# Six denser rows of quarter-array products per chunk, and V loaded behind the score blocks

## The chip, the cores and the metric

The kernel runs on one core of a Trainium2 chip. The metric is device microseconds of one execution; lower is better. Times below are medians of repeated runs, and one execution was also recorded by the hardware profiler.

## The reference

The program is a delta-rule attention block (4 batches, 8 heads, 768 tokens, head dimension 48) whose output feeds a feed-forward layer with SiLU (384 to 2048 to 384):

```python
for t in range(S):
    kt, vt, bt = (k_n[:, :, t], v[:, :, t], beta[:, :, t, None])
    y[:, :, t] = np.einsum('bhd,bhde->bhe', q[:, :, t], state)
    v_old = np.einsum('bhde,bhd->bhe', state, kt)
    state = state + bt[:, :, :, None] * np.einsum('bhd,bhe->bhde', kt, vt - v_old)
...
h = x @ w_in
g = h * (1.0 / (1.0 + np.exp(-h)))
return (g @ w_out).astype(np.float32)
```

Here `k_n` is k over its norm, and x is y with the heads side by side: 3072 tokens by 384.

## The kernel before, in words

The 768 tokens are cut into 6 chunks of 128, and each chunk into two halves of 64. All 32 heads of a chunk are worked together, in two groups g of two batches. Matrices of 64 x 64 sit in the four quarters of TensorE's array, so four small products run side by side; a product of float32 is two passes, and each pass is a weight load and a matmul, four instructions in all.

For chunk c the work is in three parts.

- `prepare(c)`, `block_steps`, `invert(c)`: `turn_blocks` (VectorE) brings k and q into transposed form, `score` (L516, with `mask`) makes the score matrices, `block_out` and `block_in` carry 32 x 32 diagonal blocks through memory into g, and `invert` inverts them on VectorE in 31 steps (L614, L619, L622). The result goes through memory again into xe and xi (`read_up`).
- `solve(c)`: `merge` (L769, 32 x 32 products) builds the rest of the inverse; per half, `keys` (L815) takes the state's prediction off V (tile vf), `inner` (L827) multiplies by the inverse into z, `old` (L893) starts the output from the state, `update` (L847) moves the state on and `new` (L906) finishes the output from z. ScalarE copies z out of the accumulators; `copy_out` and `move` bring the output into xT, the input of the feed-forward layer, partly by DMA.
- `feed_forward(c, hf)`: `hidden` (L1028) and `combine` (L1135), full-array products in half-steps of 3 or 4 matmuls. There are 60 half-steps a chunk.

[...] The last loop of the kernel alternates the parts. `go(solving)` emits the next piece of `solve`, up to its next `yield`, and `run(n)` emits n half-steps of feed-forward work of the chunk before. What stands between two `run`s is called a row here. `together` interleaves the products of its arguments one by one. All DMAs of SyncE's queue keep the order in which they are emitted (`in_line`).

The rows of `solve(c)` were: merge; keys; merge; inner and old of both groups; update and new of both groups; an empty one (copies only); keys; inner and old; update and new. `follow(c)` issues the loads of q for the next chunk, and `load_v` those of V: 8 DMAs of 96 KB. `size(c, g)` (L454) scales V on GpSimd. `lengths(c)` makes the norms of k, by squares on GpSimd and sums on VectorE.

The functions that the diff touches, and what calls them:

## Time and profile before

| what | us |
|---|---|
| median of 3 runs | 653.4 |
| their range | 652.0 to 657.42 |
| span of the profiled execution | 653.9 |
| TensorE products busy | 631.9 |
| TensorE weight loads busy | 552.0 |
| VectorE busy | 398.4 |
| ScalarE busy | 214.0 |
| GpSimd busy | 91.0 |

The span runs from the first to the last instruction of the one profiled execution. A time of its own, measured without the profiler, is not to be had, so the span is set beside the median. Chunk 0 and 1 and the weights' preparation take the first 180 us, chunks 2 to 5 the next 400, and the feed-forward layer of the last chunk the rest. Between the first merges of chunks 3, 4 and 5 pass 98.2 and 97.8 us.

### The profile page before, as it was taken

How to read it: one execution, taken by the hardware profiler on the slowest of the kernel's cores; microseconds unless marked ns; L12 is line 12 of the kernel's file. 1: busy time of each engine (PE TensorE's matmuls, PEld its weight loads, DVE VectorE, ACT ScalarE, POOL GpSimd, SP SyncE). 2: the span in 40 equal slices, each digit the busy share in tenths (PEclk: the TensorE clock that was granted, in tenths of full speed). 3: DMA queues.
4: the chain of work that ended last, by engine and by line, in shares of the span. 5: the costliest groups of instructions: out<-in, count | busy, mean ns of one | idle time of the engine just before them, and what ended most of it. 6: DMA issues, size and time to landing. Idle time of an engine off the chain costs nothing.

```text
span 653.9 us, 21366 instructions
## 1 busy us (share of the span) xinstructions
PE 631.9 (97%) x9416; PEld 552.0 (84%) x9416; DVE 398.4 (61%) x911; ACT 214.0 (33%) x497; POOL 91.0 (14%) x92
## 2 busy tenths in 40 slices
PE   7888999999999999999999999999999999999997
PEld 5576778756789988989989989989989989889997
DVE  5874689997774986443987444986444974103112
ACT  2454664332352122451122452122451122441111
POOL 5023631235101020010020010020002000000000
PEclk9968999999999998999999999999999999999999
DMA  9966634350267324167424168424073024100101
GB/s 135 211 154 191 211 72 106 97 96 3 59 146 143 62 73 60 36 142 130 79 73 59 35 146 141 63 73 60 22 148 81 2 72 60 41 13 1 25 0 25
DMA packets 145676, 54.70 MB, mean 84 GB/s; under 512 B 117152, under 2 KB 138912, under 8 KB 145584
## 3 DMA queue, kind: packets, MB, share of 16 engines
q1 hardware_dynamic: 143136, 52.93, 39.4%
q8 instruction: 74, 1.21, 0.8%
q10 hardware_dynamic: 2448, 0.41, 0.4%
q14 instruction: 18, 0.15, 0.1%
HBM read 40.14 MB, written 11.01 MB: 78 GB/s over the span
## 4 chain that ended last, share of the span: by engine, by line
PE 86%; DVE 6%; DMA 3%; issue 2%; ACT 2%; SPq 1%; POOL 0%; DVEq 0%; POOLq 0%
PE phid L1028 34%; PE px L1135 15%; PE py L1135 11%; PE po L1063 7%; PE pa L516 3%; PE pz L827 3%; DVE rank L614 2%; PE pu L847 2%; PE pyc L906 2%; PE ph L815 2%; DVE x L619 2%; PE pt L487 1%; PE pw L335 1%; PE pyc L893 1%; DMA kb<-in_k_dram 1%
## 5 line engine op out<-in xcount | busy, mean ns | idle before, releaser
L1028 PE MATMUL phid<-xT,w_in 128*128 128x256 f32 x1152 | 259.9, 383 | 1.3 <-DMA xT<-part 1.3
L1028 PEld LDWEIGHTS phid<-xT,w_in 128*128 128x128 f32 x1152 | 216.7, 191 | 33.2 <-issue 2.7
L1038 ACT ACTIVATE gT<-phid 128x512 f32<-128x512 f32 x88 | 52.6, 597 | 149.5 <-PE phid L1028 142.7
L614 DVE SCALAR_TENSOR_TENSOR rank<-g,step,x 128x31 f32<-128x31 f32 (+15 forms) x124 | 49.7, 401 | 38.0 <-DMA g<-blocks 34.6
L1117 DVE TENSOR_TENSOR sums_of_g<-gT 128x384 f32<-128x384 f32 (+1 forms) x60 | 31.7, 548 | 56.7 <-ACT gT L1038 46.1
L1135 PE MATMUL px<-sums_of_w,sums_of_g 128*128 128x192 f32 x320 | 56.8, 329 | 0.0
L1135 PE MATMUL py<-w_out,sums_of_g 128*128 128x192 f32 x320 | 56.8, 329 | 0.0
L1135 PEld LDWEIGHTS px<-sums_of_w,sums_of_g 128*128 128x128 f32 x320 | 52.2, 190 | 0.5
L1135 PEld LDWEIGHTS py<-w_out,sums_of_g 128*128 128x128 f32 x320 | 52.2, 190 | 0.4
L619 DVE TENSOR_TENSOR x<-x,rank 128x31 f32<-128x31 f32 (+15 forms) x124 | 42.5, 342 | 4.3
L454 POOL TENSOR_TENSOR vf<-vf,n_slot 128x768 f32<-128x768 f32 x10 | 15.0, 1516 | 172.6 <-DMA vf<-in_v_dram 126.9
L475 DVE STREAM_TRANSPOSE kq<-stage 128x512 f32<-128x512 f32 x28 | 28.5, 1116 | 11.1 <-DMA stage<-in_q_dram 11.1
L531 ACT COPY xT<-pyc 48x128 f32<-48x128 f32 (+2 forms) x126 | 32.7, 260 | 1.6
L1135 PE MATMUL px<-w_out,gT 128*128 128x192 f32 x160 | 29.7, 341 | 0.0
L1135 PEld LDWEIGHTS px<-w_out,gT 128*128 128x128 f32 x160 | 28.1, 200 | 0.5
L1135 PE MATMUL px<-sums_of_w,gT 128*128 128x192 f32 x160 | 28.4, 329 | 0.0
L1135 PE MATMUL py<-w_out,gT 128*128 128x192 f32 x160 | 28.4, 329 | 0.0
L827 PEld LDWEIGHTS pz<-vf,xi 64*64 64x64 f32 x768 | 25.4, 141 | 3.2 <-issue 2.9
L827 PE MATMUL pz<-vf,xi 64*64 64x48 f32 x768 | 27.0, 226 | 0.0
L1135 PEld LDWEIGHTS py<-w_out,gT 128*128 128x128 f32 x160 | 26.1, 190 | 0.3
L537 POOL COPY g<-x 64x256 f32<-64x256 f32 x4 | 5.0, 1247 | 153.3 <-DVE x L622 153.3
L1135 PEld LDWEIGHTS px<-sums_of_w,gT 128*128 128x128 f32 x160 | 26.1, 190 | 0.2
(195 smaller groups left out, 829.5 us busy)
## 6 DMA issues: line engine op xcount, KB each, us to landing
vf<-in_v_dram SPq DMA_DIRECT2D x48, 96.0 KB, 2.9
out_dram<-o SPq DMA_DIRECT2D x42, 96.0 KB, 2.2
w_out<-in_moe_w_in_dram SPq DMA_DIRECT2D x4, 768.0 KB, 4.6
sums_of_w<-in_moe_w_out_dram SPq DMA_DIRECT2D x4, 768.0 KB, 5.9
blocks<-ap SPq DMA_DIRECT2D x44, 64.0 KB, 1.9
g<-blocks SPq DMA_DIRECT2D x5, 512.0 KB, 4.1
kb<-in_k_dram SPq DMA_DIRECT2D x12, 192.0 KB, 4.8
kb<-in_k_dram SPq DMA_DIRECT2D x24, 96.0 KB, 4.3
```

The costliest lines, as they stand in the source:

```text
L454: pin(nc.gpsimd.tensor_tensor(out=vf, in0=vf, in1=of, op=ALU.mult))
L475: pin(nc.vector.transpose(out=kqs[c, b][:, :, j, :].rearrange("p a (i m) -> p a m i", i=T), in_=src.rearrange("p a (m d) -> p a m d", d=D) ...
L516: pin(nc.tensor.matmul(pa[e][half, p * n * W : (p + 1) * n * W], lhsT=kq[rows, p, 0, half], rhs=kq[rows, p, js[0] : js[-1] + 1, half], sta ...
L531: return pin(nc.scalar.copy(to, of))
L614: pin(nc.vector.scalar_tensor_tensor(out=tv, in0=g[:, 0:m, m : m + 1].to_broadcast([P, m, n]), scalar=step[:, m : m + 1], in1=x[:, m : m + ...
L619: yield pin(nc.vector.tensor_tensor(out=x[:, 0:m, m:T], in0=x[:, 0:m, m:T], in1=tv, op=ALU.add))
L827: yield pin(nc.tensor.matmul(pz[rows, n * D : (n + 1) * D], lhsT=xis[g][rows, u * H + 2 * p + e, :], rhs=vfs[c][rows, hf, g * HB + u, p, : ...
L1028: pin(nc.tensor.matmul(ph[:, j * GT : (j + 1) * GT], lhsT=w_in[:, a, (2 * f + j) * P : (2 * f + j + 1) * P], rhs=xTs[c, hf][:, a, :], star ...
L1038: pin(nc.scalar.activation(out=hidden_of(c, hf, f), in_=ph[:], func=ACTF.Silu, scale=-0.5 if in_blocks(c) else 0.5))
L1063: pin(nc.tensor.matmul(pos[i][:, 0:DM], lhsT=hidden_of(0, hf, f // 2)[:, at : at + C], rhs=w_outs[f // HFF][:, f % HFF, :], start=(f == 0) ...
L1117: pin(nc.vector.tensor_tensor(out=sums_of_g[:, k, fs], in0=of[0], in1=of[1], op=op))
L1135: pin(nc.tensor.matmul(to, lhsT=at, rhs=quarter(f, *b) if isinstance(b, tuple) else sums_of_w[b][:, f], start=start and f == 0, stop=f == ...
```

## The change

For chunks 2 to 5 `solve` makes fewer and longer rows. keys of the first half and the first merge form one row; a new function `half_chunk` puts inner and old of both groups and update and new of both groups into one row, with update and new of one group side by side in place of the same kind of both groups. The scores of all four batches are one row in place of two. The last half of chunk 5, which has no update, makes new of both groups together.

The V of the next chunk was loaded in the middle of `solve`; it is now loaded in `prepare`, behind `block_in`. `size` moves from the start of `prepare` to after the inversion. The numbers of half-steps between rows are set anew: 10 in place of 16 in `solve`, 5 in place of 4 between `solve` and the end of the scores, 12 or 14 in place of 8 or 10 behind the inversion.

```diff
+    def half_chunk(c, hf):
+
+        for g in range(2):
+            together(inner(c, g, hf), old(c, g, hf))
+        if c == NCH - 1 and hf == 1:
+            together(new(c, 0, hf), new(c, 1, hf))
+        else:
+            for g in range(2):
+                together(update(c, g, hf), new(c, g, hf))
+        copy_out()
...
+        if c > 1:
+            together(keys(c, 0, 0), keys(c, 1, 0))
+            together(merge(c, 0, False), merge(c, 1, False))
+            yield
+            together(merge(c, 0, True), merge(c, 1, True))
+            yield
+            half_chunk(c, 0)
+            yield
+            copy_out()
+            move()
+            yield
+            together(keys(c, 0, 1), keys(c, 1, 1))
+            follow(c)
+            yield
+            half_chunk(c, 1)
+            yield
+            copy_out()
+            move()
             return
...
             if hf == 1:
                 together(keys(c, 0, 1), keys(c, 1, 1))
-                if c > 1:
-                    follow(c)
                 yield
             for g in range(2):
                 together(inner(c, g, hf), old(c, g, hf))
             if hf == 1:
-                if c == 1:
-                    follow(c)
-                load_v(c + 1)
+                follow(c)
...
         if in_blocks(c):
-            for g in range(2):
-                size(c, g)
...
                     turn_blocks(c, b, 1)
-                if g == 1:
-                    for b in range(HB):
-                        scored(b)
                 yield
-            for b in range(HB, B):
+            for b in range(B):
                 scored(b)
             block_in(c)
+            load_v(c)
             yield
             return
...
-            for n in range(9):
+            for n in range(6):
                 go(solving)
-                run((2, 2, 2, 2, 1, 1, 2, 2, 2)[n])
-                if n == 5:
+                run((2, 2, 1, 1, 2, 2)[n])
+                if n == 2:
                     pieces = chained(pieces, feed_forward(c, 0), feed_forward(c, 1))
...
-            for _ in ready:
-                run(2)
-            run(6)
+            go(ready)
+            run(3)
+            go(ready)
+            run(8)
...
+            for g in range(2):
+                size(c + 1, g)
             after = lengths(c + 2) if c + 2 < NCH else iter(())
-            for _ in range(8 if c == 1 else 10):
+            for _ in range(12 if c == 1 else 14):
                 run()
-                go(after, 4)
+                go(after, 3)
```

More of the change, by code (lines that the diff above doesn't have):

```diff
@@ L984, in solve @@
             return
+        if c > 1:
[16 more added lines that the diff above has]
+            move()
+            return
         together(merge(c, 0, False), merge(c, 1, False))
```

## The prediction

> **What bounds the kernel now.** First the page: the busy shares, and the queue that carries instructions.

> ```profile
> PE 631.9 (97%) x9416; PEld 552.0 (84%) x9416; DVE 398.4 (61%) x911; ACT 214.0 (33%) x497; POOL 91.0 (14%) x92
> ...
> q8 instruction: 74, 1.21, 0.8%
> ```

> TensorE is busy 97% of the span, so only its own stream and its few waits can move the time. It runs 9416 products and 9416 weight loads, 18,832 instructions, and q8 brought them in 74 packets: 16 KB and some 256 instructions each. I come back to that.

> Second, the chain that ended last, in order of time, cut to 240 to 320 us and 343 to 400 us.

> ```profile
> 247.60 1.25 PE py L769 x80
> 248.85 4.48 PE px L1135 x16
> 254.41 2.80 PE px L1135 x16
> ...
> 312.06 2.60 PE py L1135 x16
> ...
> 363.80 1.08 PE pu L847 x64
> 364.88 0.89 PE pyc L906 x57
> 365.77 0.21 issue
> 365.98 0.34 PE pyc L906 x7
> ...
> 378.89 0.95 PE pyc L906 x64
> ```

> Sixteen full-array records of L1135 take 2.60 us among their like (312.06) and 2.80 between two rows of quarter products (254.41): a return to the full array costs 0.20. A row of 64 quarter records alone takes 1.08 (pu), a second one right behind the first 0.95 (378.89): 14.7 ns a record and 0.14 for the way in. One row more or less between full-array work is therefore 0.34 us. The merge row at 247.60 began late, and the first full-array group behind it takes 4.48 in place of 2.80. At 365.77 it waits 0.21 us for nothing but "issue".

> Third, the waits of TensorE's products in the window 195 to 580 us, chunks 2 to 5:

> ```profile
> PE py L769 <- DMA xe<-low: 1.5, 2, 0.8
> PE phid L1028 <- DMA xT<-part: 1.3, 2, 0.8
> PE pyc L906 <- issue: 0.2, 1, 0.2
> ```

> That is all there is to gain from waits: xe in chunk 2, xT in chunk 5, one "issue".

> **What the change saves.** (1) Rows. In the order of the built program a chunk had 8 rows of small products in solve and 2 of scores; it has 5 and 1. Sixteen rows less (4 x 4; chunk 5 loses 3 in solve and chunk 2 to 5 one each of scores) by 0.34 is 5.4 us. The products are the same, and kinds that follow each other cost nothing extra: pyc starts 1.08 after pu, which is the row's own length. Bound: 0 to 0.14 for keys beside merge, at most 0.6 in all; I take 0.

> (2) The xe wait of chunk 2: the merge row takes 2.11 against 1.22 in the other chunks, 0.9; another 0.9 lies before it (the full-array work there takes 51.67 for 39 half-steps of 1.30); the slow group behind it has 4.48 less 2.80, 1.7: 3.5. The half-steps of feed-forward work between scores and merge rise from 8+23+8 to 8+23+12 at c = 1, by 4 x 1.30 = 5.2 us; in the later chunks from 41 to 45. Behind xe stands the scores' way through memory, which SyncE's queue sets:

> ```profile
> 283.56 6.17 SPq L188 DMA_DIRECT2D vf<-in_v_dram  x8
> ...
> 292.43 4.11 SPq L886 DMA_DIRECT2D xT<-part  x5
> 296.64 4.28 SPq L101 DMA_DIRECT2D blocks<-ap  x8
> ```

> SyncE issues back to back from 270.98 to 300.92, so the 8 V issues (6.17 us) hold up 4 stores, 5 xT copies and 8 block writes. Behind block_in they precede only the k loads, which are wanted a chunk later. V itself is then wanted by size(), 30 us on. size() moves on GpSimd behind x L622: 2 x 1.46 us, and the four squares behind it make VectorE's sums of squares wait some 3 us; next late are sums_of_g, which feed products 6 half-steps (7.8 us) later. So it costs 0; without that cover it would be 3 a chunk.

> (3) The xT wait of chunk 5: 4.71 us for a group that is 2.80 elsewhere, 1.9. Before, the backlog shrinks by one half-step a chunk (61 run, 60 made) until chunk 5's first hidden product meets its own copies; after, it is 60 and 60 and a half chunk lies between. Gone: 1.9. (4) The issue wait at 365.77 and the row's other delay, 0.5, belong to that old order: gone.

> Saved: 5.4 + 3.5 + 1.9 + 0.5 = 11.3 us.

> **What it costs: the z copies.** inner, old, update and new now follow without feed-forward work between. ScalarE copies z for g = 0 at 360.11 for 0.48, with the row begun at 358.91; ready at 1.68, wanted when old of g = 1 ends, at 1.88. z for g = 1 ends at 2.62 and is wanted at 1.88 + 0.94 = 2.82. Both fit, by 0.2. Only in the last half, where new runs for both g at once, it is wanted at 1.88: a wait of 0.8. If ScalarE were 0.5 later (one activation in its way), each of 8 halves would lose 0.3.

> **What it costs: instructions.** These are stretches of the opening, by busy time:

> ```profile
> 37.90:40.25 2.35, 2.35 (x127) 2.25 (x128) 1.81 (x3) 1.45 (x4) 0.00 (x0) 0.50 0.74 275
> 40.25:41.73 1.48, 0.00 (x0) 0.00 (x0) 1.20 (x3) 0.36 (x1) 1.34 (x1) 0.50 0.08 18
> 52.05:55.60 3.55, 3.54 (x126) 2.79 (x127) 1.21 (x3) 1.04 (x2) 0.00 (x0) 1.00 0.65 213
> 55.60:57.19 1.59, 0.00 (x1) 0.00 (x0) 1.15 (x3) 0.42 (x1) 1.01 (x1) 1.00 0.54 98
> ```

> From the end of one "issue" wait TensorE runs 255 or 253 instructions (first two brackets: products and weight loads) and waits again, 1.48 and 1.59 us, with nothing on either of its rows. Counted in the built program, with a constant offset of 62, the three later waits (151.06, 181.54, 365.98) fall exactly on 20, 26 and 46 times 256. So TensorE holds the block it runs and one more; a dense row eats a block faster than the next arrives. From one block's first instruction to the next one's, where it waited, passed 3.83 (37.90 to 41.73), 5.14 (52.05 to 57.19), and 3.56 at the made row (362.42 to 365.98).

> A made row had 256 instructions and 32 slow ones on either side. A half_chunk has 512 in a row: 256 x 7.33 ns = 1.88 us a block. By my count the first block boundary falls 77, 138, 248, 54, 164, 225 and 79 instructions into the seven full halves, so the second always falls inside too. Its wait is the pace less 1.88. In slow stretches q8's packets start when, by my count, 46 instructions of the old block are left, 0.34 us in a dense row; so I take a pace of 3.4, just below the nearest row (3.56): 1.5 each, 10.5 in all. Bounds: 0.9 (3.56 less that lead twice, 2.9, and a tenth off) and 2.2 (the mean of 3.56 and 5.14, less the lead). Two more places: the keys-and-merge row of chunk 4 has a whole block in it (1.2 us at merge speed, 4.2 ns an instruction): 2.2; and in chunk 3 three boundaries fall from the second merge to the end of the half, 10.2 us of pace on 7.7 of work, 1.0 beyond the 1.5. Sum 13.7, bounds 8 and 20.

> [...]

> **What it costs: the clock.** Windows around three waits:

> ```profile
> 245.50:248.90 3.40, 1.89 (x131) 1.40 (x130) 2.96 (x15) 0.60 (x1) 0.00 (x0) 1.00 1.24 173
> 248.90:252.30 3.40, 3.40 (x11) 3.40 (x12) 3.22 (x10) 1.16 (x2) 0.00 (x0) 0.50 0.90 100
> 566.30:569.70 3.40, 2.14 (x10) 1.21 (x8) 1.11 (x4) 0.61 (x3) 0.00 (x0) 1.00 0.28 69
> 569.70:573.20 3.50, 3.45 (x134) 3.01 (x135) 0.00 (x0) 1.03 (x3) 0.00 (x0) 1.00 0.44 105
> ```

> With 1.51 us idle in 3.40 the granted clock (third from the end) is 0.50 in the next stretch; with 1.26 idle it stays 1.00. A wait of 1.5 is at that edge, and may be split between two stretches. Of the nine waits I let three cost it, at the 1.68 of the row at 248.85: 5.0. Bounds: 0, and seven times 1.68, 11.8. [...]

> **Sum.** -11.3 + 0.8 + 13.7 + 5.0 = +8.2. The span is 653.9; the median of the runs 653.4, so I count 0.5 off: 653.9 + 8.2 - 0.5 = 661.6, told as 661.5.

> **Rivals.** (a) The blocks arrive in time, the other side: one mechanism, instruction supply in the halves, decides at a pace of 1.9 us a block. Then -11.3 + 0.8: 643. For it: from 256 to 290 us seven boundaries pass without a wait. Against: they lie 4.6 us apart there, and the stretches from 37.90 on show what happens when they are nearer. Chance 0.12. (b) The waits come but stay near 1 us and the clock holds: -11.3 + 0.8 + 8 to 12.5: 651 to 655. For it: the opening's pace was taken beside 200 GB/s of other traffic, the halves run beside less. Against: 3.56 at 4 GB/s. Chance 0.23. (c) Nearly every wait costs clock, or loads of q beside the second halves slow the blocks: 20 + 8: 668 to 672. Chance 0.12. (d) The stream is less dense than its order says because z comes late: up to 8 x 0.3 = 2.4 on (a), 645; it would hide in the waits otherwise. Chance 0.03. The forecast, 656 to 667, keeps 0.50.

> **Numbers.** A measurement of this kernel can tell about 1% (646.9 and 659.9) from no change. Faster: (a) and (d) almost whole, 0.13. Slower: (c) and three quarters of the forecast, 0.50. Same: the rest, 0.37. The range 649 to 671 leaves out (a), (d) and some of (c); the forecast's own is 656 to 667.

> **What would show it.** Right: "issue" waits of 1 to 2 us in pu or pyc, once in each of seven halves, 333 instructions or so after its start, and one in the merge of chunk 4; no xe and no xT wait; clock of 0.50 in a few stretches; chunk period (merge to merge) near 99 us against 97.7. Each row's group of 16 still 2.80. Wrong: halves that last 3.9 us would make the instruction term 0 and the period 95.1 (97.7 less 1.3 for the half-step and 1.36 for four rows); waits on ScalarE's z in pu would mean my margin of 0.2 was none; a wait on xe would mean the block chain did not get shorter.

## The result, and the profile after

The changed kernel takes 663.31 us (median of 6 runs, 661.14 to 669.99), the kernel before in the same comparison 657.25 (652.0 to 658.92). The ratio is 1.0136, with a 95% interval of 1.0091 to 1.018: slower. The profiled execution of the changed kernel has a span of 662.1 us, 8.2 above the 653.9 of before; the two medians differ by 6.1.

The busy times and the chain's shares of the profile page, after:

```profile
PE 631.2 (95%) x9416; PEld 555.6 (84%) x9416; DVE 400.4 (60%) x911; ACT 214.3 (32%) x497; POOL 91.3 (14%) x92
...
PE 92%; issue 3%; DMA 2%; DVE 1%; ACT 1%; SPq 0%; DVEq 0%
```

TensorE is busy as long as before (631.2 against 631.9); the 8.2 us are time in which it does nothing. The waits of its products in 185 to 590 us say where (total, times, longest):

```profile
PE pu L847 <- issue: 5.4, 4, 2.0
PE pyc L906 <- issue: 3.5, 3, 1.5
PE py L769 <- issue: 2.2, 2, 1.6
PE pyc L893 <- issue: 1.1, 1, 1.1
PE pyc L906 <- ACT z L531: 0.5, 1, 0.5
```

The waits for xe and xT that led this list before are gone. Ten waits that end with nothing but "issue" stand in their place, 12.2 us in all, eight inside the halves and two in rows of keys and merge. One such wait in the chain, in the second half of chunk 2, whose row began at 272.62:

```profile
275.68 0.07 PE pu L847 x2
275.75 2.00 issue
277.75 0.20 PE pu L847
```

Products of the same row run up to it and behind it. And the clock, in windows around that wait and around the one of 1.63 us in chunk 4's row of keys and merge (the granted clock is third from the end):

```profile
275.66:279.07 3.41, 1.41 (x65) 1.25 (x60) 0.76 (x2) 2.14 (x7) 0.00 (x0) 1.00 0.73 153
279.07:282.48 3.41, 3.41 (x11) 3.23 (x11) 0.87 (x3) 0.86 (x3) 0.00 (x0) 0.50 0.78 147
...
453.15:456.56 3.41, 1.78 (x145) 1.57 (x137) 1.10 (x3) 0.00 (x0) 0.00 (x0) 1.00 0.02 5
456.56:459.97 3.41, 3.41 (x12) 3.41 (x12) 2.75 (x5) 1.49 (x3) 0.00 (x0) 0.50 0.03 7
```

Each wait is followed by 3.41 us at half clock. Between 180 and 660 us these are the only two such stretches.

### The profile page after: what moved, and what is told of

It reads as the page before. It is cut to its first block, busy times and chain, and to the rows that moved or that the text cites. A ratio compares the mean times of both kernels' runs of the same rounds, so it can differ in the third digit from the quotient of the medians.

```text
span 662.1 us, 21399 instructions
## 1 busy us (share of the span) xinstructions
PE 631.2 (95%) x9416; PEld 555.6 (84%) x9416; DVE 400.4 (60%) x911; ACT 214.3 (32%) x497; POOL 91.3 (14%) x92
## 3 DMA queue, kind: packets, MB, share of 16 engines
q8 instruction: 74, 1.21, 0.8%
## 4 chain that ended last, share of the span: by engine, by line
PE 92%; issue 3%; DMA 2%; DVE 1%; ACT 1%; SPq 0%; DVEq 0%
PE phid L1054 38%; PE px L1161 16%; PE py L1161 12%; PE po L1089 6%; PE pa L516 3%; PE pz L827 3%; PE pu L847 2%; PE ph L815 2%; PE pyc L906 1%; PE pt L487 1%; PE pw L335 1%; PE pyc L893 1%; DMA kb<-in_k_dram 1%; PE py L769 1%; PE px L769 1%
## 5 line engine op out<-in xcount | busy, mean ns | idle before, releaser
L1143 DVE TENSOR_TENSOR sums_of_g<-gT 128x384 f32<-128x384 f32 (+1 forms) x60 | 30.0, 521 | 62.2 <-ACT gT L1064 51.5
L1161 PE MATMUL py<-w_out,sums_of_g 128*128 128x192 f32 x320 | 59.8, 338 | 0.0
L1161 PEld LDWEIGHTS py<-w_out,sums_of_g 128*128 128x128 f32 x320 | 54.3, 195 | 0.4
L852 DVE TENSOR_TENSOR state<-state,pu 128x384 f32<-128x384 f32 x22 | 11.8, 552 | 32.2 <-PE pu L847 17.6
L1161 PE MATMUL px<-w_out,gT 128*128 128x192 f32 x160 | 27.6, 326 | 0.0
L526 DVE TENSOR_TENSOR ap<-pa,above 128x256 f32<-128x256 f32 x44 | 16.4, 418 | 17.6 <-ACT ap L531 13.8
L551 POOL MEMSET x<- 128x1024 f32 x4 | 3.8, 952 | 168.3 <-DMA xT<-part 75.4
L1161 PEld LDWEIGHTS px<-w_out,gT 128*128 128x128 f32 x160 | 26.6, 190 | 0.5
```

The costliest lines, as they stand in the source:

```text
L526: pin(nc.vector.tensor_tensor(out=to, in0=of, in1=above[:].unsqueeze(1).to_broadcast([P, NP, W]), op=ALU.mult))
L1143: pin(nc.vector.tensor_tensor(out=sums_of_g[:, k, fs], in0=of[0], in1=of[1], op=op))
L1161: pin(nc.tensor.matmul(to, lhsT=at, rhs=quarter(f, *b) if isinstance(b, tuple) else sums_of_w[b][:, f], start=start and f == 0, stop=f == ...
```

## The experiments

**Same rows, other block boundaries.** The edit, in the opening:

```diff
     busy(3)
+    pd = bank(CC, "pw")
+    for _ in range(48):
+        pin(nc.tensor.matmul(pd[0:T, 0:T], lhsT=ident[0:T, 0:T], rhs=ident[0:T, 0:T], start=True, stop=True))
     for b in range(B):
         square(0, b)
```

> The changed kernel with 48 products of 32x32 in the opening, whose results nobody reads: 192 TensorE instructions more ahead of everything, and nothing else. Theory 1, blocks of 256 instructions: the total of the issue waits in chunks 2 to 5 stays near 13 us, but every one moves by 192 instructions. With 3.65 us from one block to the next the row of keys and merge should wait some 2.1 us in chunk 2 (0.59 in the changed kernel) and 2.1 in chunk 5 (none there), and not in chunk 4 (1.63 there); the halves wait once each, 192 instructions earlier or 64 later in their order. Theory 2, z or any other data or position in the row: the same places and sizes as in the changed kernel, because nothing but the count ahead of them has changed. The time is within 4 us of the changed kernel's.

Measured: 667.2 us (one run), span 665.4. Of the waits of its products in 185 to 590 us:

```profile
...
PE py L769 <- issue: 3.3, 2, 1.9
PE px L769 <- issue: 1.6, 1, 1.6
...
PE pyc L906 <- ACT z L531: 0.5, 1, 0.5
```

The two waits of py are now in chunk 2 (1.4 us, expected 2.1) and chunk 5 (1.9, expected 2.1), and chunk 4, which had 1.63, has none. Nothing but the count of instructions ahead of the row has changed, so the place of these waits follows that count. The halves say it to the instruction. This is the number of product records that ran in a row before its wait:

| row (first and second: the halves) | changed kernel | shifted |
|---|---|---|
| chunk 2, keys and merge | 136 | 168 |
| chunk 2, first | 165 | 197 |
| chunk 2, second | 197 | 229 |
| chunk 3, first | 123 and 251 | 155 |
| chunk 3, second | 155 | 187 |
| chunk 4, first | 209 | 241 |
| chunk 4, second | 241 | 145 |
| chunk 5, first | 167 | 199 |
| chunk 5, last (waits for z) | 130 | 130 |

A record of a product has a weight load beside it (9416 of each), so 32 records later are 64 instructions, and 96 earlier are 192: the shift, modulo 256. The only wait on data, z in the last half, stays where it was, at 0.5. So neither z nor a fixed place in the row makes the others. From the start of the second half of chunk 4 to its wait, changed and then shifted (products alone; each count has one record of the full-array work before):

```profile
476.64:480.41 3.77, 3.77 (x242) 1.00 0.74 163
...
477.53:479.80 2.27, 2.27 (x146) 1.00 0.39 95
```

Not as foreseen: this half waits only 0.12 us in the shifted run, where I expected a wait in each of the seven, and 1.6 us are lost in the second merge of chunk 5, right behind the other. With pu (4.5), pyc (4.0) and a full-array product behind a row (0.9) the total is 14.3, not 13.

**The suspected cost by itself.** The kernel before, with a probe row in the four inversions:

```diff
+                if n == 12:
+                    pds = [bank(A, "pw"), bank(CC, "pw")]
+                    for i in range(128):
+                        i1, i2 = i % 2, i // 2 % 2
+                        i3 = slice(W * (i // 4 % 8), W * (i // 4 % 8) + W)
+                        i4 = HALVES[i1]
+                        pin(nc.tensor.matmul(
+                            pds[i2][HALVES[i1 ^ i2], i3], lhsT=ident[i4, i4], rhs=ident[i4, i4],
+                            start=True, stop=True, skip_group_check=True,
+                        ))
+                    run()
...
-            for _ in range(8 if c == 1 else 10):
+            for _ in range(7 if c == 1 else 9):
```

In the second version `if i == 64: run()` stands in the loop in place of the `run()` behind it.

> The kernel before with a probe: once in each of the four inversions, between two half-steps, 128 products of 64x64 on the identity into two banks, in one row: 512 TensorE instructions that wait for no data and that nobody reads. Theory 1, blocks: each of the four rows takes 128 x 14.7 ns = 1.9 us x 2 = 3.8 us plus one wait for nothing but issue of 1.2 to 1.8 us in it. Theory 2, the waits of the halves came from z or from copies: no wait in any probe row, 3.8 us each.

> The same probe, cut into two rows of 64 products (256 instructions) with one half-step of full-array work between. Theory 1: no issue wait over 0.4 us in any of the eight rows; each takes 1.9 to 2.0 us with its way in. The time is under that of the probe in one row by some 4 x (1.5 + 0.3) less 4 x 0.34, 6 us, and by up to 1.7 more for each stretch of half clock that the waits bring. Theory 2: no difference but the four rows more, 1.4 us slower.

Measured: 683.37 us in one row (span 681.4), 673.52 in two (span 671.6), one run each. The chain through the first probe, in one row:

```profile
225.61 2.94 PE pw L1524 x186
228.55 1.37 issue
229.91 1.27 PE pw L1524 x67
```

and cut in two:

```profile
220.43 2.02 PE pw L1526 x128
222.46 1.50 PE py L1135 x8
223.96 2.02 PE pw L1526 x128
```

The four long rows wait 1.37, 1.31, 0.90 and 1.13 us and last 5.1 to 5.6; of the eight short ones seven last 2.02 or 2.03 and one 2.19, with no wait. Nothing here waits for data. One half-step of 1.50 us between them was enough. Two of the four waits lie in the 1.2 to 1.8 expected, two below it. The difference of the times, 9.9 us, holds waits in the opening too (5.6 against 1.5 us in pl L733), which fell otherwise in these two executions and which I do not explain.

The traces hold two more signs of the same cause. In the eleven profiles (both kernels and all experiments) TensorE's products wait 120 times, behind 30 us and for over 0.15 us, for nothing but issue. Counted in the trace (products, weight loads and the sequencer's records of TensorE, and the same 63 added in every run), the instruction behind each of these 120 waits has a number that is a multiple of 256; not one of the 74 waits for another engine or a DMA stands at such a place. And each of the 120 ends 1.19 to 1.81 us after a packet of 16 KB on the instruction queue q8 had ended, while the waits on data end 1.2 to 25 us after one.

**The halves cut in two.**

```diff
-            half_chunk(c, 0)
+            half_inner(c, 0)
+            yield
+            half_outer(c, 0)
...
-                run((2, 2, 1, 1, 2, 2)[n])
-                if n == 2:
+                run((2, 2, 1, 1, 1, 2, 1, 1)[n])
+                if n == 3:
...
-            for _ in range(12 if c == 1 else 14):
+            for _ in range(11 if c == 1 else 13):
```

The same cut is made in the second half; `half_inner` and `half_outer` are the two parts of `half_chunk`.

> The changed kernel, but each half of chunks 2 to 5 is cut into two rows again: inner with old (256 instructions), one half-step of feed-forward work, then update with new (256). 60 half-steps a chunk as in the changed kernel, 11 of them in solve. Theory 1, instruction blocks: no stretch of a half is longer than a block any more, so the eight waits for nothing but issue inside the halves (10.0 us in the profile of the changed kernel) go or stay under 0.4 us each, with the 0.3 us by which each stretched its row besides and one of the two stretches of half clock; what stays is the wait in the row of keys and merge, about 0.6 us in chunk 2 and 1.6 in chunk 4, the latter with its stretch of half clock. Eight rows more at 0.34 us cost 2.7. So some 11 us less than the changed kernel's 663.3: 651 to 654, faster than before by 0.5 to 1%. Theory 2, the halves are late because of z, the copies between their own four kinds of products: the half-step covers the copy too, so the waits go as well; this run alone does not tell the two apart, but the shifted run beside it does. Theory 3, the waits are only a small part and the loss is the clock's: the time stays within 3 us of 663.

Measured: 655.78 us (650.1 to 659.51), ratio to before 1.0002 (0.9964 to 1.0039), span 656.1. The waits in 185 to 590 us:

```profile
PE py L769 <- issue: 3.4, 3, 2.3
PE pu L847 <- issue: 0.6, 2, 0.4
PE pyc L906 <- issue: 0.5, 1, 0.5
```

As expected the halves' waits all but vanish, and with them the loss against before. The time is some 2 us above the expected 651 to 654: I had taken the waits of keys and merge as they were, 0.6 and 1.6, and they are 0.77 in chunk 2, 2.30 in chunk 4 and 0.30 in chunk 5, because a half-step more or less ahead of a row moves its boundary; and the waits of chunks 2 and 4 are each followed by a group of 16 at 4.47 and 4.48 us, half clock, where I expected one.

**V where it was.** `load_v(c + 1)` back in `solve`, `load_v(c)` out of `prepare`.

> The changed kernel with V loaded where the kernel before loaded it, ahead of the scores of the next chunk, so that its eight issues on SyncE stand before the stores, the xT copies and the score blocks again. Theory 1: the move matters only for chunk 2, where the blocks' way through memory was late by 0.9 us before with 39 to 41 half-steps of cover; with 45 to 43 now it is covered with or without V in the queue, or a wait for xe of under 1 us shows in chunk 2 and none in chunks 3 to 5. The time is within 3 us of the changed kernel's. Rival: V's place is what removed the xe wait: then the row of keys and merge waits for xe by 2 us or more in chunk 2, at some 3.5 us with the clock.

Measured: 663.44 us (one run), span 661.5; no wait for xe in any chunk, and the same issue waits within 0.7 us a group. V's place does not matter to the changed kernel.

**The old rows with the other parts of the change.** `half_chunk` and its branch are taken out again, and the half-steps are

```diff
-                run((2, 2, 1, 1, 2, 2)[n])
-                if n == 2:
+                run((2, 2, 2, 2, 1, 1, 2, 2, 2)[n])
+                if n == 5:
...
-            for _ in range(12 if c == 1 else 14):
+            for _ in range(6 if c == 1 else 8):
```

> The rows of solve as in the kernel before (eight rows a chunk, no half_chunk; 16 half-steps between them), with all other parts of the change: V behind the score blocks, size behind the inversion, one row of scores, 60 half-steps a chunk. Theory 1, instruction blocks in the long rows are the whole loss: no issue wait over 0.5 us in chunks 2 to 5, no wait for xe in chunk 2 (V no longer holds up the score blocks, 6.2 us of SyncE's queue, against one half-step less behind the scores), none for xT in chunk 5. Against the kernel before: 3.5 (xe, with its clock) + 1.9 (xT) + 1.4 (four score rows) less, 657.3 - 6.8 = 650 to 652. Rival: the parts outside the rows cost something of their own (size late on GpSimd, V late): then 656 or more, with waits for sums_of_g, vf or xe in the trace.

Measured: 659.29 us (655.79 to 663.16), ratio to before 1.0087 (1.0054 to 1.0119): slower, where I expected faster. In its profile, span 654.5, one of its quickest executions, the waits in 185 to 590 us are

```profile
PE py L769 <- DMA xe<-low: 4.9, 5, 2.3
PE px L1133 <- issue: 0.6, 1, 0.6
```

The issue waits went as expected, and xT's too. But xe is late in all four chunks now, by 2.35 and 0.70 us in chunk 2 and 0.43 to 0.74 in the others. SyncE's queue in chunk 3:

```profile
291.44 4.66 SPq L101 DMA_DIRECT2D blocks<-ap  x8
...
340.86 0.92 SPq L637 DMA_DIRECT2D xe<-low  x2
```

The blocks went out 5.2 us earlier than before (296.64), but VectorE's inversion ended only 2.8 earlier (334.88 against 337.67), while the merge row began 3.7 earlier (343.32 against 347.01): 16 half-steps between the rows leave 39 behind the scores, 50.9 us, where the changed kernel has 45. So my step "no wait for xe" had a condition that I had told only in part: the cover that hides xe is what the shorter solve left over. Seven of the ten executions take 658 to 663, at granted clocks of 0.976 to 0.986; what they lose besides is open.

**Old rows, fewer half-steps between.** Against the last kernel:

```diff
-                run((2, 2, 2, 2, 1, 1, 2, 2, 2)[n])
-                if n == 5:
+                run((2, 2, 2, 1, 1, 1, 2, 2, 0)[n])
+                if n == 4:
...
-            for _ in range(6 if c == 1 else 8):
+            for _ in range(9 if c == 1 else 11):
...
     busy(3)
+    pd = bank(CC, "pw")
+    for _ in range(7):
+        pin(nc.tensor.matmul(pd[0:T, 0:T], lhsT=ident[0:T, 0:T], rhs=ident[0:T, 0:T], start=True, stop=True))
```

> The rows of solve as before (eight a chunk, none over 256 instructions), the other parts of the change, but 13 half-steps between the rows in place of 16 (2, 2, 2, 1, 1, 1, 2, 2, 0 behind the nine steps), so that 42 half-steps lie between scores and merge (40 in chunk 2) where the run with the old rows had 39 (37); and seven products of 32x32 in the opening that nobody reads, 28 instructions, which put the block boundaries where my count of the rows gives no wait. Theory: two things cost the change and the run with the old rows their gain, the blocks in long rows and the half-steps taken from xe's cover. From the end of the score row to xe's landing some 51.4 us passed with the old rows; 42 half-steps are 54.7, 40 are 52.1. So no wait for xe (under 0.3 in chunk 2), none for xT, no issue wait over 0.5, no stretch of half clock behind 200 us: the kernel before less 3.5 (xe) less 1.9 (xT) less 1.4 (four rows), 654.5 - 6.8 = 647 to 649. Rival: the old rows with V late lose for another reason (size late, V late): xe waits again, or others in its place, 654 or more.

> The run with 13 half-steps between the old rows, but V loaded where the kernel before loads it, ahead of the scores. What V's place is worth by itself: in the changed kernel with V early the score blocks went out 4.6 us behind the start of the score row, with V late 2.7: 1.9 us later. Against a margin of 3.3 us in chunks 3 to 5 and 0.6 in chunk 2: a wait for xe of about 1.3 us in chunk 2 with its stretch of half clock, none in the others, some 3 us in all. Rival: V's eight issues hold the blocks up by their whole 6.2 us: waits of 3 us in chunks 3 to 5 as well, 12 us or more.

Measured: 653.92 us (652.97 to 657.19), ratio 1.003 (1.0003 to 1.0057), span 651.5; with V early 654.89 (one run), span 653.1. In chunks 2 to 5 no wait for xe, xT or issue is left in the first of them; what its list has is new:

```profile
PE phid L1026 <- ACT gT L1036: 3.9, 4, 1.1
```

The 0 at the end of my list was a mistake: with no half-step behind the last products of a chunk, ScalarE does the copies of both groups at once, and the hidden products wait 0.9 to 1.1 us for its activation, once a chunk. That leaves the time 5 us above the forecast of 647 to 649. With V early there is no wait for xe either, so both my 1.3 us and the rival fall. The blocks' read into g was issued at 204.54 with V early and 199.76 with V late, 4.8 us apart, but the write of low behind the inversion at 239.70 and 238.42, only 1.3 apart: the inversion between them began 4.2 us later with V early and took 30.2 us in place of 33.2. Why it took less I did not look into.

**The end mended.** One line more:

```diff
-                run((2, 2, 2, 1, 1, 1, 2, 2, 0)[n])
+                run((2, 2, 2, 1, 1, 1, 2, 1, 1)[n])
```

> The run with 13 half-steps and the seven products, with one figure of the list changed: 1 and 1 half-steps behind the last two rows of a chunk in place of 2 and 0. In that run nothing lay between the last products and their copies, so ScalarE did all 16 copies at once and the products of hidden waited four times for its activation, 0.9 to 1.1 us each, 3.9 in all. Theory: with a half-step between, the copies of the second group come one by one as in the changed kernel, these four waits go, and nothing takes their place: 3.9 us less than that run, 649 to 651, against 654 of before. Rival: the four waits only move (the copies are late for the next thing, xT or the hidden chain of the next half): 653 to 655.

Measured: 651.64 us (648.01 to 652.51) against 654.91 of before, ratio 0.9927 (0.9899 to 0.9955), span 648.3. That is faster than the kernel before by 0.7%, and 2.3 us below the version with the 0, where I expected 3.9; the upper end of the forecast, 651, is just missed. What the seven idle products are worth by themselves was not run. All the waits of its products from 185 to 640 us:

```profile
PE pu L847 <- issue: 0.4, 1, 0.4
PE pyc L906 <- issue: 0.2, 1, 0.2
```

## Why the prediction was right

**Bound.** Right: TensorE's busy time did not move, and the difference is in its waits.

**What was saved.** The prediction says 11.3; the spans say about 10.3. The costs below come to 19.1, and the spans differ by 8.2, but the opening, up to 187 us the same work in both, happened to take 0.6 less in the changed kernel's execution, so that behind it 8.8 are lost. The waits for xe and xT are gone. The score rows give what was priced: one row of 3.65 against two of 1.91 and a return of 0.20, 0.37 a chunk. The row of keys and merge, where not made to wait, takes 2.29, no less than 1.08 and 1.22 apart, so it saves the return of 0.20 and not 0.34: 0.5 less over four chunks, near the far end of the bound of 0.6 of which I had taken 0. What removed the xe wait was not V, as part (2) has it with its 6.17 us: with V early it stays away. It was the 45 half-steps (43 in chunk 2): with V late and 39 (37) xe waited in all four chunks, and with 42 (40) it did not wait, with V early or late.

**z.** Right: in the seven full halves no wait for z shows; in the last half the wait is 0.48, forecast 0.8. That the margin of 0.2 held for the second group is shown by three halves only, whose wait for instructions comes behind the first use of its z (197, 209 and 241 records in, z at 192); in the other four an earlier wait for instructions could have hidden it.

**Instructions.** Right in kind and in place, nearly in size: 12.2 us, forecast 13.7 with bounds of 8 and 20. The second boundaries that I had counted, 256 behind 77 to 248 instructions, lie 155 to 252 records into the halves, and the table in the section on the experiments has the waits within two records of each. Behind the start of the halves at 261.08, 272.62, 361.32, 375.21, 464.87, 476.64 and 563.39 the waits are 0.68, 2.00, 1.54, 1.07, 0.94, 1.78 and 0.91: 1.27 on average, not 1.5. The extra of chunk 3 is 1.15 (forecast 1.0), the row of chunk 4 1.63 (2.2). The 0.59 in the same row of chunk 2 I had not foreseen. In the second halves the waits are longer (2.00, 1.07, 1.78, beside 130 to 144 GB/s of DMA traffic) than in the first halves with one wait (0.68, 0.94, 0.91, beside 4 or 5); whether the traffic makes them longer, as rival (c) has it, no run here separates. Each wait, though, costs more than its idle time, which the sum left out. The same row of half 1 of chunk 4 took 5.93 with a wait of 1.78 in the changed kernel and 4.28 with 0.12 in the shifted one: 4.15 and 4.16 once the wait is taken off, where 256 records at 14.7 ns and 0.14 for the way in make 3.9; the half of chunk 3 with two waits lasts 0.6 longer than its records and waits. So about 0.27 a wait is lost besides, however short it is, 3.0 for these ten and the one on z; what takes it is open.

**Clock.** Two stretches and not three: 3.4 us, not 5.0. With the rest: 12.2 + 3.0 + 3.4 + 0.5 = 19.1, against 0.8 + 13.7 + 5.0 = 19.5. The 3.0 that was missed and the 1.5, 1.6 and 0.3 that were priced too high cancel; that the spans differ by just the forecast 8.2 is luck.

**Period.** I gave 99 us from merge to merge as a sign. It was 101.05, 99.98 and 102.09, so mine was too low. The terms as measured give it: 95.1 and 0.14 for the row of keys and merge, the waits in between, 0.27 for each and 1.7 for each stretch of half clock make 101.0, 99.8 and 102.1.

**From the span to the time.** I took the median of 653.4 as 0.5 below the span. The recorded times lie 1.7 above their spans (663.78 with 662.1), and before's median came out at 657.25 in this comparison and 654.1 to 654.9 in the later ones: that is the 1.8 by which 661.5 is low. The range held, and so did the mechanism; that the miss is so small is luck again.

**Rivals.** (a), blocks in time, 643, is out: the probe shows the wait with nothing else in the row. The version with the end mended, whose rows have up to 256 instructions, has 0.6 us of issue waits behind 185 us; the long rows of the changed kernel have 12.2. (b) was nearer in the size of the single wait (1.27 against my 1.5), and 12.2 lies within its 8 to 12.5, but the clock did not hold. (c) is out: two stretches, not seven. (d) is out, z was on time. The granted clock was 0.50 behind 2.00 us idle of 3.41, and behind 1.63.

## What to carry to other kernels

Count instructions, not products, before rows of small work are joined: a row past a block of 256 paid about 1.3 us and 0.27 besides for each crossing here, several times the 0.34 us that a row more costs, and one half-step of full-array work, 1.5 us, after 256 instructions brought the wait to nothing in the probe and under 0.5 us in the halves. Where two streams share an engine, work taken out from between the rows of the one is cover for the other's transfers: the best version here kept the old rows of solve and had three half-steps fewer between them and three more behind the scores than the version that waited for xe. And since each of the 120 issue waits here stood at a multiple of 256, read the place of such a wait from the trace, then test by shifting everything with a few idle instructions.

## What was not expected of the hardware

Half clock followed less idle time in stretches of 32x32 products (0.77 us) than in stretches of 64x64 (2.00), and the length of a wait alone did not tell it. A stretch here has 3.41 us: in the traces of both kernels any two changes of the granted clock lie a whole number of 3.41 us apart (279.07 and 456.56 in the changed kernel, 52 of them), and these changes give the bounds of the other stretches.

Among stretches with 64x64 products, those with 2.00 and 2.02 us of TensorE idle (changed and shifted, the second half of chunk 2) were followed by half clock, and those with 1.86 and less were not. The 2.30 of the halves cut in two, in a stretch with 28 records of a merge, was followed too. Behind the shifted run's wait of 2.24 and the 2.09 with V early there was no half clock: a bound splits them, and the larger part left 1.86 and 1.28 idle in one stretch. Among stretches with at least 100 records of a merge's 32x32 products, half clock followed 0.77 us of idle time (halves cut in two, chunk 2), 1.19 (shifted), 1.20 (V early), 1.51 (before), 1.63 (changed) and 1.63 (old rows). It did not follow 0.70 (old rows), 0.90 (shifted) and 1.12 (the probe cut in two), so idle time alone does not tell it there; what else does stays open. The shifted run's two merge waits in chunk 5, 1.88 and 1.59, were not followed by it either: their stretches hold 22 and 89 of these records, with 1.55 and 1.22 idle.
